# Three chained layers on one core: attention of the first token blocks spread over the matrix product's halves, old outputs copied out through the probabilities' buffer, weight pieces split in place

## The chip, the cores and the metric

The kernel runs on one core of a Trainium2 chip. The metric is the device time of one execution in microseconds (us), lower is better. Of a profiled execution the span (first to last instruction) is given too; the profile's times are counted from the span's start. The engines are PE (matrix products; PEld is its weight loading), DVE (VectorE), ACT (ScalarE), POOL (GpSimd) and SP (SyncE, which issues all DMAs of this kernel). Each engine takes its instructions strictly in the order of its own queue.

## The reference

```
q, k, v: (8, 8, 576, 64)                       # batch, heads, sequence, head size
k_p, v_p = means of k and v over groups of 8 in the sequence      # 72 rows a head
attn = softmax(q @ k_p.T / sqrt(64))           # 576 x 72 a head
x = (attn @ v_p), heads side by side           # 4608 tokens x 512
x = (sigmoid(x @ w_gate) * (x @ w_val)) @ w_out            # inner width 1536
h = x @ w_in2                                  # inner width 2048
out = where(h > 0, h, exp(min(h, 0)) - 1) @ w_out2         # 4608 x 512, float32
```

The inputs come as float64. The kernel narrows the weights to float32 with integer operations on VectorE, and keeps each float32 number as a high part (what TensorE takes) and a low rest, so that one product is three passes: high x high, high x low, low x high.

## The kernel before, in words

All of it is one function in which instructions are written in the order in which each engine takes them (the order is by hand; nothing is rescheduled). 4608 tokens are nine blocks of 512, each of four query tiles of 128. The stages, with names that the text uses:

**Stage 1 (begin).** Attention of block 0. For a query tile t: `emit_q` transposes the queries on PE and ACT copies them out; `emit_s` makes the scores on PE and `off_peak` subtracts each row's maximum on DVE (two instructions); `emit_exp` is ACT; `emit_norm` sums and inverts on DVE and scales on POOL; `emit_t` transposes the probabilities on PE, and ACT and DVE split them into `pt` (one buffer for the block). `emit_pv` multiplies them with the pooled values (`weighted`) and splits the result into `x`. `emit_k` and `sums_of` pool and place keys and values. Between these stand calls of `convert(1)`: one conversion is four DVE instructions on 128x512 (lines 109, 113, 119 and 123) that narrow one weight tile, an ACT absolute value (line 205) for the next one, and a split (ACT, then POOL, lines 96 and 97) of one before.

**Stage 2.** The loop over c = 0..5 of the first gated layer for block 0: a gate product (`emit_gate`, 12 matmuls), its sigmoid, a value product (12), `emit_g` (multiply on DVE, split), and for the c before, the output product (`emit_y`, 12). Three conversions lie in each c, and the attention of block 1 lies around the products. Every step of that attention takes the same pair of PSUM banks (`two_banks`, one buffer): scores, transposed queries and transposed probabilities wait for each other's readers. At its end `emit_pv(1)` makes `x` of block 1.

**Stage 3.** c = 6..11 of block 0, with block 1's gate and value products of two c's (`side_gate`, `side_val`) in each. `work(n)` lets a background generator (`form_weights`, then `prepared`) go on by n steps.

**Stage 4.** The output product of block 1, j = 0..9 (12 matmuls each), and the attention of block 2 around it, placed by `put2`; the last weight forms are stored. It ends with `weighted` of block 2.

**Stage 5.** Blocks 2 to 8 in a form with seven smaller products for eight: u = 0..11, each with seven steps k = 0..6 of six matmuls on 128x256. After each step some matmuls of the output product follow (`filler`), then what `thin_plan` put at (u, k): the attention of the next block in single banks (`q_thin`, `s_thin`, `t_thin`). `work()` is called at the places of `WORK_AT` (35 a block) and narrows the second layer's weights (`prepared`): tiles `a`, `b`, `c` of the tag `nt` (three buffers) and raw tiles of the tag `raw` (two buffers), which are stored to DRAM. `flush_one` copies the finished output of the block before to DRAM through the row tiles (three buffers, which the loads of q, k and v take too).

**Stage 6.** The second layer; PE is busy throughout, and the change doesn't touch it.

Of the kernel before, what the change touches and what calls it, by code (L numbers as in the profile page):

```python
# [24 lines left out]
def fused_kernel(  # L25
# [260 lines left out]
    def prepared():  # L286
# [21 lines left out]

        def store(d, place):
            nc.sync.dma_start(out=place, in_=f32(d))  # L310
# [17 lines left out]
        for q in range(C2 // 2):  # L328
# [31 lines left out]
            fetch(i + 3)  # L360
            yield
        last = None
        for i in range(C2, len(loads)):
            steps = narrowing(i)
            next(steps)
            if last is not None:
                store(last, wo2_dram[i - 1 - C2])
            yield
            next(steps)
            yield  # L370
            next(steps)
            if last is not None:
                fetch(i + 1)
            yield
            yield from steps
            last = halved(raws[i], tiles[i].bitcast(F32))
            yield
            magnitude(i + 1)
            yield
        yield  # L380
        yield
        store(last, wo2_dram[C2 - 1])
# [384 lines left out]
    def plan():  # L767


        early, pre, mid, post = [[[] for _ in range(C1)] for _ in range(4)]  # L770
        for i in range(TPW):
            t = TPW + i
            pre[1 + i].append(lambda t=t: (t, emit_s(t)))
            mid[2 + i].append(lambda t=t: emit_t(t))
        for i in range(TPW):
            pre[i].append(lambda t=TPW + i: emit_q(t))
        post[0].append(lambda: sums_of("v", 1))
        for c in range(NCH):
            post[(1, 1, 2, 3, 4)[c]].append(lambda c=c: place_v(1, c))
# [7 lines left out]
        return early, pre, mid, post  # L787

    with tc.manual_schedule():
# [51 lines left out]
        for c in range(NCH):  # L841
            pool_k(0, c)
        emit_k(0)
# [4 lines left out]
        open_to(2)  # L848
        scored(0)
        convert(1, 0, 0)  # L850
        scored(1)
        scored(2)
        emit_norm(0, ph[0])
        scored(3)
        emit_norm(1, ph[1])
        sums_of("v", 0)
        emit_t(0)
# [3 lines left out]
        convert(1, 1)  # L861
        emit_t(1)
# [3 lines left out]
        emit_t(2)  # L866
        sums_of("k", 1)
        convert(1, 1)
        emit_t(3)
        emit_pv(0)  # L870
        emit_k(1)
# [6 lines left out]
        early, pre, mid, post = plan()  # L878
# [10 lines left out]
        def side_gate(c):  # L889
            sg = at_p.tile([P, NW], F32, name="sg1", tag="qT" if c % 2 else "p")  # L890
            nc.scalar.activation(out=sg, in_=side(c, 0), func=AF.Sigmoid)
            return c, sg
# [8 lines left out]
        for c in range(C1):  # L901
            for f in early[c]:
                f()
            late = c >= LAG_FROM
            second = 2 * (c - LAG_FROM)
            later = [f for f in [op() for op in pre[c]] if f]
            gps = emit_gate(x0, c, 0)
            sg = emit_sig(gps)
            for f in later:
                emit_exp(f[1])  # L910
            convert(1)
            work(3)
            if late:
                one = side_gate(second)
            for op in mid[c]:
                op()
# [3 lines left out]
            for f in later:  # L920
                emit_norm(*f)
            for op in post[c]:
                op()
            if late:
                side_val(*one)
            convert(1)
            work(4)
# [5 lines left out]
            if late:  # L933
                side_val(*side_gate(second + 1))
                work(3)
                formed[0] = second // 2 + 1
            if c == LAG_FROM - 1:
                emit_pv(1)
                wide.close()
                lag_ps.append(lag.enter_context(tc.tile_pool(name="ps_lag", bufs=1, space=PSUM)))  # L940
# [16 lines left out]

        again(C1 - 2)
        while stores:
            stores.pop(0)[1]()  # L960
        reload(0)
        emit_k(SQ)
        emit_y(0, *pend)
# [5 lines left out]
        t0 = SQ * TPW  # L969
        emit_q(t0)  # L970
# [6 lines left out]
        at2 = [[] for _ in range(C1)]  # L977

        def put2(c, f, *a):
            at2[c].append(lambda: f(*a))  # L980
# [3 lines left out]
        def s2(t):  # L984
            p = raw_tile("p2").rearrange("p f w -> p (f w)").bitcast(F32)[:, :HK]
            p2[t] = emit_s(t, p)
            emit_exp(p)

        for i in range(TPW):
            t = t0 + i  # L990
            put2(2 * i, s2, t)
            put2(2 * i + 1, lambda t=t: emit_norm(t, p2[t]))
            if i + 1 < TPW:
                put2(2 * i, load_q, t + 1)
                put2(2 * i + 1, emit_q, t + 1)
            put2(2 * i + 3, emit_t, t)
        for c in range(NCH):
            put2((1, 2, 3, 4, 5)[c], load_kv, "k", SQ + 1, c)
            put2((4, 5, 6, 7, 8)[c], pool_k, SQ + 1, c)
        put2(8, emit_k, SQ + 1)  # L1000
        put2(9, load_q, t0 + TPW)
        for j, c in enumerate(order[:-2]):
            if j % 2 == 1:
                reload(j // 2 + 2)
            for f in at2[j]:
                f()
            y = y_steps(acc, g_of[c], c, wo[C1 + c], first=j == 0, last=False)
            for f in y:
                f()
# [3 lines left out]
            work(2)  # L1013
# [71 lines left out]
        a2 = two_banks("atv")  # L1085
# [563 lines left out]
```

## Time and profile before

| | us |
|---|---|
| runs, median of 3 (lowest to highest) | 1947.32 (1945.09 to 1948.89) |
| the profiled execution | 1951.63 |
| its span | 1949.9 |
| PE busy / DVE busy / ACT busy / POOL busy | 1812.7 / 1097.3 / 858.4 / 638.4 |
| stages 1, 2, 3, 4 | 58.9, 116.1, 119.9, 63.8 |
| stage 5, seven blocks | 131.6, 117.2, 118.8, 117.7, 114.3, 113.8, 112.2 |
| stage 6 | 765.7 |

The stages follow each other without overlap on PE, whose queue sets their order, so the span is their sum. PE is busy for 93% of the span; what it isn't busy, 137 us, lies nearly all in stages 1 to 5. A busy PE may also be a slow one: its clock has two levels, and the column PEclk of a window is the mean share of full speed that was granted in it.

### The profile page before, as it was taken

Reading aid. Unit: us, or ns where it says so; the run is one execution under the profiler, and the core shown is the slowest. Engines: PE = TensorE matmul, PEld = TensorE weight load, DVE = VectorE, ACT = ScalarE, POOL = GpSimd, SP = SyncE. Lnnn points to the kernel's source line nnn. Section 1 sums busy time; section 2 is a strip of 40 time slices with the busy share of each in tenths; the row PEclk is TensorE's granted clock in tenths of the full one; section 3 lists DMA queues with packets and bytes.
Section 4 is the critical chain, followed back from the end, with each engine's and each line's share of the span. In section 5 each row is a group of like instructions: output and inputs, shape, how many; then the busy total and the mean of one; then the engine's idle time right before and its main releaser. Section 6 shows DMA issues by size and latency. Waiting matters only on the chain. (4 is left out here: it accounts for less than half of the span.)

```text
span 1949.9 us, 28296 instructions
## 1 busy us (share of the span) xinstructions
PE 1812.7 (93%) x10308; PEld 1604.7 (82%) x10308; DVE 1097.3 (56%) x2053; ACT 858.4 (44%) x1775; POOL 638.4 (33%) x626
## 2 busy tenths in 40 slices
PE   5668997898999999999999999999999999999999
PEld 4556876688888888888889788999999999899898
DVE  6667985576676667766666554434444344443432
ACT  3343333344444444545444334444454444444443
POOL 2333564333334343333332322222222222222222
PEclk8778998899999999999999999999999999999999
DMA  8234545576676766666576786334343353343431
GB/s 221 90 114 131 195 159 190 202 232 206 218 231 204 253 211 211 222 230 224 179 250 209 267 291 260 130 121 171 114 178 114 116 190 126 131 172 133 146 114 52
DMA packets 158618, 351.29 MB, mean 180 GB/s; under 512 B 49168, under 2 KB 87056, under 8 KB 158480
## 3 DMA queue, kind: packets, MB, share of 16 engines
q1 hardware_dynamic: 158480, 349.48, 52.5%
q8 instruction: 82, 1.34, 0.3%
q14 instruction: 56, 0.46, 0.1%
HBM read 289.14 MB, written 60.29 MB: 179 GB/s over the span
## 5 line engine op out<-in xcount | busy, mean ns | idle before, releaser
L1480 PE MATMUL bank<-form,wr 128*128 128x384 f32 x2016 | 411.0, 338 | 1.0 <-DVE u L1513 0.7
L1480 PEld LDWEIGHTS bank<-form,wr 128*128 128x128 f32 x2016 | 366.5, 188 | 29.1 <-DVE u L1513 1.1
L717 PE MATMUL acc<-g,wos 128*128 128x512 f32 x1128 | 367.7, 409 | 22.5 <-ACT g L96 20.0
L1526 PE MATMUL oacc<-w2o,gc 128*128 128x512 f32 x1080 | 288.9, 393 | 0.4 <-POOL gc L97 0.4
L1526 PEld LDWEIGHTS oacc<-w2o,gc 128*128 128x128 f32 x1080 | 199.6, 187 | 30.4 <-POOL gc L97 0.8
L717 PEld LDWEIGHTS acc<-g,wos 128*128 128x128 f32 x1128 | 191.0, 195 | 39.3 <-ACT g L96 26.1
L97 POOL TENSOR_TENSOR gc<-ea,gc 128x384 fp32r<-128x384 f32 x96 | 98.1, 1022 | 298.5 <-ACT gc L96 293.2
L97 POOL TENSOR_TENSOR gc<-pair,gc 128x384 fp32r<-128x384 f32 x96 | 98.0, 1021 | 260.4 <-ACT gc L96 240.0
L1359 PE MATMUL pl<-s,wg 128*128 128x256 f32 x1008 | 155.4, 290 | 15.2 <-DVE u L1374 14.8
L1359 PEld LDWEIGHTS pl<-s,wg 128*128 128x128 f32 x1008 | 142.6, 192 | 31.9 <-DVE u L1374 16.5
L97 POOL TENSOR_TENSOR g<-sg,g 128x512 fp32r<-128x512 f32 x98 | 129.8, 1341 | 102.2 <-ACT g L96 102.0
L1359 PE MATMUL pl<-a,wg 128*128 128x256 f32 x1008 | 152.3, 287 | 6.6 <-ACT u L1369 4.1
L1359 PEld LDWEIGHTS pl<-a,wg 128*128 128x128 f32 x1008 | 142.0, 192 | 19.0 <-ACT r L1063 4.9
L1359 PE MATMUL pl<-s,tt 128*128 128x256 f32 x1008 | 153.9, 289 | 3.5 <-DVE u L1398 2.8
L1359 PEld LDWEIGHTS pl<-s,tt 128*128 128x128 f32 x1008 | 138.9, 191 | 12.2 <-DVE u L1398 3.9
L1526 PE MATMUL oacc<-w2p,gc 128*128 128x512 f32 x540 | 143.1, 393 | 0.0
L96 ACT ACTIVATE g<-sg 128x512 fp32r<-128x512 f32 x98 | 61.6, 628 | 151.0 <-DVE sg L1399 117.8
L1526 PEld LDWEIGHTS oacc<-w2p,gc 128*128 128x128 f32 x540 | 99.8, 187 | 14.8
L1489 ACT ACTIVATE ea<-bank 128x384 f32<-128x384 f32 x48 | 23.6, 492 | 157.3 <-PE bank L1480 157.3
L1493 DVE SCALAR_TENSOR_TENSOR ea<-ea,bank 128x384 f32<-128x384 f32 x48 | 26.6, 555 | 117.2 <-ACT ea L1490 117.2
L1394 POOL TENSOR_TENSOR sg<-sg,u 128x256 f32<-128x256 f32 x42 | 36.0, 858 | 162.6 <-DVE u L1393 162.6
L688 PE MATMUL gv<-x,wg 128*128 128x512 f32 x288 | 80.5, 436 | 3.6 <-DVE x L97 3.6
(225 smaller groups left out, 3075.9 us busy)
## 6 DMA issues: line engine op xcount, KB each, us to landing
wr<-wd SPq DMA_DIRECT2D x96, 896.0 KB, 6.5
tt<-td SPq DMA_DIRECT2D x84, 768.0 KB, 4.5
wos<-wd SPq DMA_DIRECT2D x94, 512.0 KB, 5.5
rw<-in_moe_w_out_dram SPq DMA_DIRECT2D x22, 512.0 KB, 3.9
td<-tw SPq DMA_DIRECT2D x36, 256.0 KB, 4.2
r<-yd SPq DMA_DIRECT2D x24, 384.0 KB, 8.2
out_dram<-po SPq DMA_DIRECT2D x36, 256.0 KB, 2.0
rw<-in_moe_w_in_dram SPq DMA_DIRECT2D x16, 512.0 KB, 6.2
```

Of the source, the lines that this page charges most:

```text
L96: nc.scalar.activation(out=dst_hi, in_=src, func=AF.Copy)
L97: eng.tensor_tensor(out=dst_lo, in0=src, in1=f32(dst_hi), op=ALU.subtract)
L688: nc.tensor.matmul(d, lhsT=w[:, i, a_w, j], rhs=x[j][:, a_x], start=(j == 0 and a_w == 0 and a_x == 0), stop=(j == KD - 1 and a_w == 1),)
L717: return lambda: nc.tensor.matmul(acc[m], lhsT=w[:, a_w, m * P:(m + 1) * P], rhs=g[:, a_g], start=(first and a_w == 0 and a_g == 0), stop= ...
L1359: nc.tensor.matmul(src, lhsT=w(a_w, j), rhs=f_t[nm][:, j, a_x], start=opens and m == 0, stop=m == 5, skip_group_check=True,)
L1394: nc.gpsimd.tensor_tensor(out=c22, in0=c22, in1=u4, op=ALU.mult)
L1480: nc.tensor.matmul(bank[b ^ flip], lhsT=wp[q][a_w][:, w, j * P:(j + 1) * P], rhs=form_tile(s, a)[j][:, a_x], start=opens and n == 0, stop= ...
L1489: nc.scalar.activation(out=e, in_=src, func=AF.Relu, scale=-1.0)
L1493: nc.vector.scalar_tensor_tensor(out=e, in0=e, scalar=-1.0, in1=src, op0=ALU.add, op1=ALU.max)
L1526: return lambda: nc.tensor.matmul(acc[t + i], lhsT=g[c][:, a_g, i * P:(i + 1) * P], rhs=wo2[2 * q + e][a_w], start=opens and p == 0, stop= ...
```

## The change

Six edits, named E1 to E6 in what follows.

**E1, stage 1.** The conversions move: one goes ahead of the keys' transposes, one behind the transposed probabilities, and one of five leaves the stage. All four score tiles come first, then the norms, then all four `emit_t`. `emit_k(1)` goes to stage 2.

**E2, stage 2.** The loops for c < 6 and c >= 6 are written apart. In c the order on PE is now: scores of tile t, gate, transposed probabilities of tile t-1, value, transposed queries of t+1, output. The output product of c = 5 follows `emit_pv(1)` and leaves stage 3.

**E3, stage 4.** A step j is cut into two halves of six matmuls, and `put2` places the attention by halves: queries, scores, exp, norm and transposes of a tile stand in different halves. The `weighted` products of block 2 move behind three more output matmuls, and what follows them (`form_x`) is spread over u = 0 as for the later blocks, no longer finished ahead of it.

**E4, stage 5, attention.** Nearly all of `thin_plan` moves one step k earlier; queries and values are loaded three to seven steps earlier than before.

**E5, stage 5, old outputs.** `flush_one` writes into a tile of the tag `pt`, which lies idle then, no longer into row tiles, and begins at (0, 3), before (0, 6).

**E6, `prepared`.** Splits of `c`, of `a`'s half and of the output weights are made in place (`apart`: the high part goes into another `nt` tile, the rest stays where the number was), where a raw tile took both parts. Each such piece is stored by two DMAs where one did it (24 more in all); raw tiles are fetched earlier. `WORK_AT` has 40 places a block, before 35.

```
+        def apart(x, r):
+            split(x.bitcast(F32R), r.bitcast(F32R), r)
...
-            dc = halved(raw_tile("rs2"), c)
             yield
             store(do, part(q, 1))
-            yield
-            store(dc, part(q, 2))
-            da = halved(raw_tile("rs2"), a[:, hi])
-            yield
+            apart(b, c)
+            yield
+            apart(a[:, lo], a[:, hi])
             fetch(i + 2)
             yield
-            store(da, part(q, 3, 1))
+            for n, x in enumerate((b, c)):
+                nc.sync.dma_start(out=w_dram[q][:, n, 4:6].rearrange("p a f -> p (a f)"), in_=x)
+            yield
+            nc.sync.dma_start(out=part(q, 3, 1), in_=a.rearrange("p (s f) -> p s f", s=2))
+            fetch(i + 3)
+            yield
             yield
             yield
             magnitude(i + 2)
-            fetch(i + 3)
             yield
...
+            fetch(i + 2)
+            last = plain_t().bitcast(F32), tiles[i].bitcast(F32)
+            apart(*last)
...
+        for c in range(LAG_FROM):
+            t = TPW + c - 1
+            p = emit_s(t) if 0 < c <= TPW else None
             gps = emit_gate(x0, c, 0)
+            if p is not None:
+                emit_exp(p)
             sg = emit_sig(gps)
             convert(1)
+            if c == 0:
+                emit_k(1)
+            elif c == 1:
+                sums_of("v", 1)
+            elif c <= TPW + 1:
+                emit_t(t - 1)
+            if p is not None:
+                emit_norm(t, p)
             vps = emit_gate(x0, c, 1)
             convert(1)
             g = emit_g(sg, vps)
             for op in post[c]:
                 op()
+            if c < TPW:
+                emit_q(t + 1)
             if pend is not None:
                 emit_y(0, *pend)
...
+        emit_pv(1)
+        emit_y(0, *pend)
...
+        for i, (hq, hs, ht) in enumerate(((0, 0, 5), (2, 3, 10), (7, 8, 15), (12, 13, 19))):
             t = t0 + i
+            if i:
+                put2(hq, emit_q, t)
+                put2(hq - 2, load_q, t)
+            put2(hs, s2, t)
+            put2(hs + 1, lambda t=t: emit_exp(p2[t]))
+            put2(hs + 2, lambda t=t: emit_norm(t, p2[t]))
+            put2(ht, emit_t, t)
...
-        filler(9)
-        for _ in shapes:
-            pass
...
+        filler(3)
+        d = places[:2] + [one_bank("atv")[:, 0, :], places[2]]
+        weighted(SQ, d)
+        shapes = form_x(SQ, d)
+        next(shapes)
+        filler(7)
...
-                put(u, 6, q_thin, t)
-                put(u + 1, 0, s_thin, t, 0)
-                put(u + 1, 2, s_thin, t, 1)
+                put(u, 5, q_thin, t)
+                put(u, 6, s_thin, t, 0)
+                put(u + 1, 1, s_thin, t, 1)
...
-                put(u, 0, load_q, t)
+                put(*((u - 1, 4) if i else (1, 1)), load_q, t)
...
-                        flush_one(n - 1, prev_acc, FLUSH_AT.index((u, k)), row_tile("yo"))
+                        m = FLUSH_AT.index((u, k))
+                        if m == 0:
+                            flushed = wts.tile([P, KD, NW], F32, name="yo", tag="pt")
+                        flush_one(n - 1, prev_acc, m, flushed[:, m])
+                        if m == KD - 1 and n + 1 < NWB:
+                            pt_now[0] = new_pt()
```

PE's queue in stage 2, one c, before (ats: scores, atq: transposed queries, att: transposed probabilities, gv: gate or value product, acc: output product):

```order
L574 MATMUL ats<-kbd_140,qT 128x144 x4
L566 MATMUL atq<-ident,q_173 128x128 x4
L688 MATMUL gv<-x,wg_738 128x512 x12
L628 MATMUL att<-ident,p_711 128x128 x4
L628 MATMUL att<-ident,pl 128x128
L688 MATMUL gv<-x,wg_738 128x512 x12
L717 MATMUL acc<-g,wo_683 128x512 x12
```

The same place now:

```order
L580 MATMUL ats<-kbd_140,qT 128x144 x4
L694 MATMUL gv<-x,wg_646 128x512 x12
L634 MATMUL att<-ident,p_572 128x128 x4
L634 MATMUL att<-ident,pl 128x128
L694 MATMUL gv<-x,wg_646 128x512 x12
L572 MATMUL atq<-ident,q_173 128x128 x4
L723 MATMUL acc<-g,wo_592 128x512 x12
```

Between any two steps that take the pair of banks there are now twelve matmuls of another kind; before, the transposed queries followed the scores directly.

PE's queue in stage 4, j = 2 and 3, before (wos: output weights):

```order
L717 MATMUL acc<-g,wos_2219 128x512 x12
L628 MATMUL att<-ident,p_2223 128x128 x4
L628 MATMUL att<-ident,pl 128x128
L566 MATMUL atq<-ident,rq 128x128 x4
L717 MATMUL acc<-g,wos_2221 128x512 x12
L574 MATMUL ats<-kbd_139,qT 128x144 x4
```

The same place now:

```order
L723 MATMUL acc<-g,wos_2219 128x512 x6
L634 MATMUL att<-ident,p_2223 128x128 x4
L634 MATMUL att<-ident,pl 128x128
L723 MATMUL acc<-g,wos_2219 128x512 x6
L723 MATMUL acc<-g,wos_2221 128x512 x6
L572 MATMUL atq<-ident,rq 128x128 x4
L723 MATMUL acc<-g,wos_2221 128x512 x6
L580 MATMUL ats<-kbd_139,qT 128x144 x4
```

Transposed probabilities and transposed queries stood side by side and have twelve matmuls between them now.

ACT's queue in stage 5 where `prepared` splits a piece, before (rw, rs: raw tiles; nt: narrowed tiles; u: the copy of the step k = 0 that the next products' sums need):

```order
L96 ACTIVATE rw_2817<-nt 128x512
L1387 ACTIVATE sg<-sg 128x256
L96 ACTIVATE rs_3202<-nt 128x512
L1390 ACTIVATE sg<-sg 128x512
L1146 ACTIVATE qT<-atq 128x512
L1369 ACTIVATE u_2750<-pl_2747 128x256
L501 ACTIVATE vhl<-vs 128x64
L1152 ACT_TABLE_LOAD
L1152 ACTIVATE idle<-idle 128x1
L600 ACTIVATE p<-p 128x576
L96 ACTIVATE rs_3291<-nt 128x256
```

The same place now:

```order
L96 ACTIVATE rw_2822<-nt 128x512
L1406 ACTIVATE sg<-pl_2637 128x256
L1409 ACTIVATE sg<-sg 128x256
L1167 ACTIVATE qT<-atq 128x512
L96 ACTIVATE nt<-nt 128x512
L1412 ACTIVATE sg<-sg 128x512
L96 ACTIVATE nt<-nt 128x256
L1391 ACTIVATE u_2640<-pl_2637 128x256
```

The splits of the second kind write `nt`, no longer a raw tile `rs` whose store has to land first.

## Rows read from the trace of the kernel before

**Rows 1.** Windows by stage: stages 1 to 4, blocks 2, 3, 7 and 8.

```profile
core 0: us, PE busy (x) PEld busy (x) DVE busy (x) ACT busy (x) POOL busy (x), PEclk, DMA share, GB/s
0.00:58.90 58.90, 34.13 (x170) 27.40 (x171) 33.89 (x58) 20.85 (x47) 15.36 (x27) 0.90 0.68 183
58.90:174.95 116.05, 78.75 (x358) 64.67 (x357) 81.98 (x116) 50.55 (x83) 43.98 (x34) 0.81 0.38 125
174.95:294.82 119.87, 117.60 (x505) 96.17 (x505) 93.95 (x132) 42.34 (x86) 63.42 (x56) 0.98 0.48 159
294.82:358.61 63.79, 49.32 (x210) 39.34 (x211) 36.17 (x59) 22.61 (x49) 27.04 (x23) 0.87 0.62 208
358.61:490.20 131.59, 117.28 (x778) 104.40 (x777) 82.15 (x171) 56.43 (x125) 45.73 (x49) 0.94 0.65 209
490.20:607.41 117.21, 109.78 (x770) 98.91 (x769) 82.83 (x170) 54.98 (x122) 44.48 (x46) 1.00 0.66 219
...
958.22:1072.02 113.80, 109.41 (x766) 98.95 (x765) 70.43 (x158) 53.55 (x109) 36.77 (x33) 1.00 0.63 213
1072.02:1184.20 112.18, 104.98 (x682) 94.93 (x681) 64.09 (x134) 38.23 (x86) 34.71 (x30) 0.95 0.77 275
```

**Rows 2.** Timeline of PE, stages 1 to 3; brackets: idle before, releaser.

```profile
48.47 0.49 PE L650 MATMUL atv<-pt,vbd 128*128 128x512 f32 x1 [1.80 <-ACT pt L96]
...
97.84 1.08 PE L566 MATMUL atq<-ident,q 128*128 128x128 f32 x4 [8.37 <-issue]
...
120.24 1.09 PE L566 MATMUL atq<-ident,q 128*128 128x128 f32 x4 [10.18 <-issue]
...
174.95 5.45 PE L688 MATMUL gv<-x,wg 128*128 128x512 f32 x12 [3.56 <-DVE x L97]
...
188.42 2.88 PE L717 MATMUL acc<-g,wo 128*128 128x512 f32 x12
```

**Rows 3.** Timeline of DVE, stages 1 and 2.

```profile
21.47 0.76 DVE L586 TENSOR_REDUCE mx<-ats 128x8 f32<-128x576 f32 x1 [6.46 <-PE ats L574]
...
23.54 0.42 DVE L109 TENSOR_SCALAR nt<-nt 128x512 f32<-128x512 f32 x1
...
107.28 0.69 DVE L97 TENSOR_TENSOR pt<-att,pt 128x512 fp32r<-128x512 f32 x1 [7.66 <-ACT pt L96]
...
119.38 0.76 DVE L587 TENSOR_TENSOR p<-ats,mx 128x576 f32<-128x576 f32 x1
```

**Rows 4.** Timeline of ACT, stage 2.

```profile
103.71 1.28 ACT L600 ACT_TABLE_LOAD   x1
...
106.67 0.58 ACT L96 ACTIVATE pt<-att 128x512 fp32r<-128x512 f32 x1
```

**Rows 5.** Groups by line, DVE, stage 2: count, busy us, mean ns, idle before.

```profile
L109 DVE TENSOR_SCALAR nt<-nt 128x512 f32<-128x512 f32 x15 | 13.7, 911 | 8.6 <-ACT nt L205 8.6
L113 DVE TENSOR_SCALAR nt<-nt 128x512 int32<-128x512 int32 x15 | 11.0, 731 | 0.0
L123 DVE SCALAR_TENSOR_TENSOR nt<-rwo,nt 128x512 int32<-128x512 int32 x9 | 8.1, 895 | 0.0
L119 DVE SCALAR_TENSOR_TENSOR nt<-rwo,nt 128x512 int32<-128x512 int32 x9 | 6.2, 684 | 0.1
```

**Rows 6.** Timeline of PE, block 2.

```profile
372.33 1.65 PE L1359 MATMUL pl<-a,wg 128*128 128x256 f32 x6 [4.12 <-ACT u L1369]
...
484.57 1.65 PE L1359 MATMUL pl<-s,wg 128*128 128x256 f32 x6 [3.66 <-DVE u L1374]
```

**Rows 7.** Timeline of ACT, block 2.

```profile
483.37 0.42 ACT L96 ACTIVATE rs<-nt 128x256 fp32r<-128x256 f32 x1 [5.63 <-DMA wd<-rw]
```

**Rows 8.** Waits of ACT, stage 5: total us, times, longest.

```profile
ACT rs L96 <- DMA wd<-rw: 19.2, 7, 5.6
...
ACT yo L749 <- DMA yd<-yo: 15.1, 4, 6.6
```

**Rows 9.** Waits of SP's queue, stage 5.

```profile
SPq L1024 <- PE pl L1359: 334.5, 68, 11.6
...
SPq L128 <- DMA wd<-rs: 36.1, 8, 7.5
```

**Rows 10.** Timeline of SP, block 8: the issue of one store.

```profile
1094.50 0.49 SPq L310 DMA_DIRECT2D wod<-rw  x1
```

More of the change, by code (lines that the diff above doesn't have):

```diff
@@ L359, in prepared, with keep @@
             magnitude(i + 2)
-            fetch(i + 3)
             yield
         last = None
+        def keep(i, x, y):
+            for n, z in enumerate((x, y)):
+                nc.sync.dma_start(out=wo2_dram[i - C2][:, n], in_=z)
         for i in range(C2, len(loads)):
@@ L366, in prepared @@
             if last is not None:
-                store(last, wo2_dram[i - 1 - C2])
-            yield
[L369 to L373, printed above, removed]
+                keep(i - 1, *last)
             yield
             yield from steps
-            last = halved(raws[i], tiles[i].bitcast(F32))
+            fetch(i + 2)
+            last = plain_t().bitcast(F32), tiles[i].bitcast(F32)
+            apart(*last)
             yield
@@ L381, in prepared @@
         yield
-        store(last, wo2_dram[C2 - 1])
+        keep(len(loads) - 1, *last)
     def background():
@@ L847, in fused_kernel @@
                 emit_q(t, qt[:, t], a[:, t - i, :])
[L848 to L855, printed above, removed]
+        for t in range(TPW):
+            scored(t)
+            if t > 1:
+                emit_norm(t - 2, ph[t - 2])
         sums_of("v", 0)
-        emit_t(0)
         emit_norm(2, ph[2])
@@ L865, in fused_kernel @@
             place_v(0, c)
-        emit_t(2)
+        for t in range(TPW):
+            emit_t(t)
+        convert(1, 1)
+        emit_pv(0)
         sums_of("k", 1)
[L868 to L871, printed above, removed]
         convert(1)
@@ L932, in fused_kernel @@
             pend = acc, g, c
[L933 to L940, printed above, removed]
+            convert(1)
+        emit_pv(1)
+        emit_y(0, *pend)
+        pend = None
+        wide.close()
+        lag_ps.append(lag.enter_context(tc.tile_pool(name="ps_lag", bufs=1, space=PSUM)))
+        for c in range(LAG_FROM, C1):
+            for f in early[c]:
+                f()
+            second = 2 * (c - LAG_FROM)
+            sg = emit_sig(emit_gate(x0, c, 0))
+            convert(1)
+            work(3)
+            one = side_gate(second)
+            vps = emit_gate(x0, c, 1)
+            convert(1)
+            g = emit_g(sg, vps)
+            for op in post[c]:
+                op()
+            side_val(*one)
+            convert(1)
+            work(4)
+            if pend is not None:
+                emit_y(0, *pend)
+            pend = acc, g, c
+            side_val(*side_gate(second + 1))
+            work(3)
+            formed[0] = second // 2 + 1
         lag.close()
@@ L956, in reload, with prep @@
                 back[2 * k], back[2 * k + 1] = t[:, 0], t[:, 1]
+        def prep(n=1):
+            for _ in range(n):
+                if stored[0] < C1:
+                    work()
         again(C1 - 2)
@@ L961, in fused_kernel @@
         reload(0)
+        t0 = SQ * TPW
         emit_k(SQ)
-        emit_y(0, *pend)
+        y = y_steps(pend[0], pend[1], pend[2], wo[pend[2]])
+        for f in y[:6]:
+            f()
+        emit_q(t0)
+        for f in y[6:]:
+            f()
         reload(1)
@@ L1083, in form_x @@
             yield
-        a2 = two_banks("atv")
-        d = [ps.tile([P, NW], F32, name="xv", tag="gv", bufs=2) for _ in range(2)] + [a2[:, 0, :], a2[:, 1, :]]
-        weighted(SQ, d)
-        shapes = form_x(SQ, d)
         fill = []
```

112 lines of the change are left out of this document (40 added, 72 removed).

## Prediction

> **What bounds the kernel now.** I read the windows by stage first: they tell where PE isn't busy and how fast its clock was. In stage 2 PE is busy for 78.75 of 116.05 us and the granted share is 0.81; in stage 4 it is 49.32 of 63.79 at 0.87; block 2 has 14.3 us of idle at 0.94, block 3 has 7.4 at 1.00, block 7 has 4.4, and block 8 has 7.2 at 0.95 [rows 1]. No other engine is full there: DVE has 82 us of work in stage 2, 36 in stage 4 and 82 in block 3. So these stages are bound by neither PE nor another engine, but by hand-overs between them. Stage 6 is PE without a gap, and the change leaves it alone.
>
> Then the timelines, for what ends the long waits. In stage 2 the transposed queries wait 8.37 and 10.18 us [rows 2]: they take the pair of banks that holds the scores, whose last reader on DVE starts at 119.38 and ends at 120.14 [rows 3], behind two conversions. PE stands with a gate product queued right behind. DVE is starved in its turn: at 107.28 it had waited 7.66 us for ACT, and ACT for PE. The two wait for each other once in each c. In block 2 PE waits 4.12 us for the first copy of ACT and 3.66 us at 484.57 [rows 6]; just before the latter ACT had waited 5.63 us for a store out of a raw tile [rows 7]. That wait comes 7 times in stage 5, 19.2 us together, and the copies of old outputs wait 15.1 us in 4 for their row tiles' stores [rows 8].
>
> **Stage 1 (E1).** A conversion is 0.91 + 0.73 + 0.90 + 0.68 = 3.2 us of DVE at stage 2's means [rows 5]; undisturbed, line 109 takes 0.42 rather than 0.91 [rows 3], so I put a conversion alone at twice 0.68 + 0.42, 2.2. Three conversions lay between the first scores (21.47) and the weighted sums (48.47) [rows 2, 3]. One moves ahead of the keys' transposes. I cost it at nothing: DVE sat idle 6.46 us before the first scores [rows 3]; without that cover it costs 2.2. One goes behind the transposed probabilities, beside PE's weighted sums; one goes to stage 2. The chain loses 6.6 to 9.7 us of DVE, of which the four splits of probabilities, now back to back with ACT between, take some. I take **-5.4**; bounds 0 and -9.7.
>
> **Stage 2 (E2).** Work is the same but for one key placement; DVE's 82 us are the floor and 116 the ceiling. What stays is one hand-over a c. When PE has transposed, ACT must first do what stands ahead: from the table load at 103.71 to the split at 106.67 it was 3.0 us [rows 4]. The 8 and 10 us waits go, since a gate or value product (2.88 us for twelve matmuls, [rows 2]) now lies between any two users of the banks. With some 3 us of starved DVE in each of six c's, 82 + 18 = 100, and 2 more for the last weighted sums and splits before stage 3: 102, so **-14**. It is nearer to the floor because the conversions that PE waited for now run while PE multiplies. Bounds -34 and 0.
>
> **Stage 3.** One output product (2.88 us) moves into the 3.56 us in which PE waited for `x`, and the first gate, 5.45 us after that wait, may run as the 2.88 of the later ones [rows 2]. DVE gets a conversion more (3.2 on 93.95 of 119.87, [rows 1]). **-4**; bounds 0 and -9.
>
> **Stage 4 (E3).** PE's 49.32 busy us at a granted 0.87 are about 43 at full clock [rows 1]. Its idle 14.5 us stand at transposes and scores that follow a sibling directly; these now have six or twelve matmuls between them. The transfers set a second floor: 208 GB/s for 63.8 us are 13.3 MB, and at block 8's 275 GB/s [rows 1] that is 48 us. I take 53, between the floor of 48 and the old time and nearer the floor, **-11**; bounds 0 and -16.
>
> **Block 2 (E3).** Its beginning becomes that of the later blocks, so its time becomes block 3's: 131.59 - 117.21 [rows 1] gives **-14**. The wait of 4.12 us and the slow clock behind it (1.65 us for six matmuls, at both long waits, [rows 6]) are what goes. The upper bound on the gain is block 7's time, -18; the lower, if the long wait at 484 us stays with what it costs in clock, -8.
>
> **Blocks 3 to 7 (E4, E5, E6).** Idle is 7.4 in block 3 and 4.4 in block 7. The store waits of ACT (rs and yo) go with their tiles, and SP's queue stands no longer for 36.1 us behind stores before it may fetch [rows 9], which let loads of queries and weights come late. In their place, the absolute value that follows a pair must now wait for the stores out of `nt`; there are three `work` steps between, where there was one. The 24 stores more cost 0.49 us of SP each [rows 10], 12 us in all; they are hidden because SP waits 334.5 us in stage 5 for PE to free a weight buffer [rows 9], and uncovered they would cost those 12 at most. Attention moves as a whole by one step, so its own spacing is kept. The preparing gets 40 steps for 35 a block and needs about 246 (seven more than before), so it ends with block 7; that makes earlier blocks denser on DVE by a seventh of the preparing. I take **-7** over five blocks; bounds +8 and -16.
>
> **Block 8.** Preparing leaves it; it had the largest share of DMA (0.77 at 275 GB/s, [rows 1]) and 7.2 us of idle, where block 7 has 4.4. **-4**; bounds 0 and -8.
>
> **Sum.** 5.4 + 14 + 4 + 11 + 14 + 7 + 4 = 59.4 us. The profiled execution took 1951.63 us (span 1949.9), so 1892.2 for such a one; it lay 4.3 above the median of the runs, so **1888 us**.
>
> **A rule against it.** DVE's instructions in stage 2 are longer than alone (0.91 for 0.42, [rows 5, 3]) while POOL works 43.98 us there. The Trainium skill, SBUF — State Buffer, section Who interferes with whom, says that a VectorE instruction with two SBUF inputs and a GpSimd one that reads SBUF exclude each other for their whole length. The trace agrees as far as that more than doubling goes. If all of POOL's work shut out all of DVE's, the floor of stage 2 would be 44 us plus DVE's undisturbed time, not 82: by my count 18 conversions of 2.2, four tiles of 3.7 (five instructions near 0.75) and some 8 of multiplications and splits, 62; together 106. I don't take it, since the instructions that read PSUM (subtracting the maximum, 0.76 in [rows 3], as the reduction before it in stage 1) show no lengthening.
>
> **Rivals.** (a) *DVE and POOL exclude each other:* stage 2 comes to 106 and, with the hand-overs left, to 114; stage 3's denser DVE eats its 4. Then -2 for -18: 1904. For it: DVE is busy 94 of 120 us in stage 3. Against it: DVE was idle for 34 us of stage 2, and the rows on that name ACT (7.66 once, 8.6 ahead of line 109, [rows 3, 5]). (b) *The blocks gain nothing:* the denser preparing costs what the tiles give, block 2 keeps its wait at 484 us: -8 for -25 over stage 5, 1905. For it: blocks with the heavy half of preparing are 3.4 us longer than block 7 [rows 1]. (c) *Slower:* ACT waits for stores out of `nt` as it did for raw tiles. There are 8 + 16 such pieces; the old wait was 19.2 / 7 = 2.7 us [rows 8]. If each holds ACT and PE with it, 24 x 2.7 = 65 us are lost and the result is about 1953; it decides from 2.5 us of PE a piece. Against it: three to five steps of slack for one, and PE lost only 3.66 of ACT's 5.63 us in the worst case. (d) *The order doesn't matter:* PE's waits go over to DVE's queue in all of stages 1, 2 and 4, as the conversions stay in order ahead of the subtractions; then -30 of -59 go, 1918.
>
> **Chances.** Forecast 0.62 (1870 to 1898), (a) 0.14, (b) 0.12, (d) 0.07, (c) 0.05. About 0.2% (4 us) is what a measurement of this kernel tells from no change. Faster 0.93, same 0.02, slower 0.05. The range reaches from 1866 (stage 2 near its floor, stage 4 at 48) to 1918, where (c) and the better tail are left out.
>
> **What would show it.** Stage 2 at 100 to 105 us with waits at transposed queries below 3 us, and DVE's wait for `pt` below 4; the first weighted sums at 43 us; stage 4 at 50 to 55 with no wait over 2 us; block 2 within 2 us of block 3; no ACT wait for a store at the copies of old outputs, and few at `nt`; block 8 with no fetch of output weights. The prediction is wrong if stage 2 stays over 110, or if ACT's waits for stores of `nt` exceed 20 us in stage 5.

## The result, and the profile after

The changed kernel takes 1871.92 us (median of 4 runs, 1869.42 to 1873.26); the kernel before took 1946.2 beside it (4 runs, 1939.94 to 1948.89). The ratio is 0.9621, 95% interval [0.9596, 0.9647]: 74 us faster, where 59 were forecast. 1888 was too high by 16 us; the time lies inside the range, near its lower end. The profiled execution took 1872.07 us, its span is 1869.8.

Windows by stage after, cut as in [rows 1]: stages 1 to 4, blocks 2, 3 and 8.

```profile
0.00:51.33 51.33, 32.37 (x161) 25.79 (x161) 29.86 (x55) 18.59 (x43) 11.51 (x25) 0.90 0.78 210
51.33:154.46 103.13, 82.32 (x378) 65.97 (x378) 79.88 (x115) 51.33 (x86) 45.85 (x34) 0.87 0.38 125
154.46:269.96 115.50, 112.69 (x493) 92.03 (x493) 98.97 (x136) 43.33 (x88) 65.92 (x57) 1.00 0.55 179
269.96:327.83 57.87, 43.94 (x214) 34.61 (x214) 38.39 (x60) 22.97 (x51) 27.68 (x24) 0.94 0.70 230
327.83:446.39 118.56, 111.10 (x775) 99.80 (x774) 79.06 (x170) 57.15 (x125) 44.48 (x49) 0.97 0.71 239
446.39:557.03 110.64, 108.80 (x770) 98.97 (x769) 82.42 (x174) 55.06 (x122) 43.64 (x46) 1.00 0.71 237
...
998.35:1104.13 105.78, 101.85 (x682) 92.42 (x681) 56.40 (x120) 33.59 (x78) 27.99 (x27) 0.98 0.70 256
```

The differences are -7.6, -12.9, -4.4 and -5.9 for stages 1 to 4, -13.0 for block 2 and -6.4 for block 8. Blocks 3 to 7 together, the sum row of the same five windows, before and then after:

```profile
sum 581.82, PE 549.61 PEld 493.89 DVE 391.38 ACT 273.88 POOL 210.75; mean PE 109.92 PEld 98.78 DVE 78.28 ACT 54.78 POOL 42.15
```

```profile
sum 551.96, PE 543.68 PEld 494.07 DVE 392.74 ACT 275.73 POOL 214.11; mean PE 108.74 PEld 98.81 DVE 78.55 ACT 55.15 POOL 42.82
```

That is -29.9. The seven numbers make -80.1, which is the span's 1949.9 - 1869.8; it is more than the 74 of the medians because the profiled execution of before was a long one. In blocks 3 to 7 PE's idle time (sum less PE busy) fell from 32.2 to 8.3 us, that is by 23.9; the other 5.9 is busy time for the same matmuls, and no row here says why it fell.

What ended PE's idle in those blocks, before (20 waits for ACT's split of `g`, the gated product):

```profile
PE acc L717 <- ACT g L96: 14.4, 20, 1.0
PE pl L1359 <- DVE u L1374: 6.7, 10, 1.4
PE atq L1145 <- DMA rq<-in_q_dram: 3.4, 4, 1.0
```

After, in the same blocks, 0.3 us of the first kind and none of the third is left:

```profile
PE pl L1381 <- DVE u L1396: 3.8, 4, 1.6
PE pl L1381 <- DVE xe L1078: 2.1, 5, 0.4
...
PE acc L723 <- ACT g L96: 0.3, 2, 0.2
```

Of the long waits that remain elsewhere, three matter in what follows. In stage 2, after's rows of PE, then of ACT, answer to [rows 2, 4]:

```profile
100.13 2.29 PE L580 MATMUL ats<-kbd,qT 128*128 128x144 f32 x8 [3.69 <-ACT qT L573]
```

```profile
98.96 0.63 ACT L96 ACTIVATE g<-sg 128x512 fp32r<-128x512 f32 x1 [4.00 <-DVE sg L712]
99.50 0.58 ACT L573 ACTIVATE qT<-atq 128x512 f32<-128x512 f32 x1
```

The scores wait for the copy of the queries, which stands on ACT behind a split that itself waits for DVE. It comes four times, 14.2 us together (longest 4.3). In stage 4, the timelines of SP (DMA issues) and PE:

```profile
274.20 4.75 SPq L760 DMA_DIRECT2D yd<-yo  x8
...
280.01 0.39 SPq L427 DMA_DIRECT2D rq<-in_q_dram  x1
```

```profile
286.77 1.08 PE L572 MATMUL atq<-ident,rq 128*128 128x128 f32 x4 [6.24 <-DMA rq<-in_q_dram]
```

PE waits 6.24 us for one query tile, whose load was issued behind eight stores of old outputs and two weight loads. In block 2, DVE waits for keys and PE for DVE:

```profile
357.16 1.01 DVE L483 TENSOR_REDUCE ks<-rkv 128x64 f32<-128x512 f32 x1 [4.70 <-DMA rkv<-in_k_dram]
```

```profile
358.56 1.65 PE L1381 MATMUL pl<-s,wg 128*128 128x256 f32 x6 [6.05 <-DVE u L1396]
```

### The profile page after: what moved, and what is told of

Its sections match the earlier page's. It is cut to its first block, busy times and chain, and to the rows that moved or that the text cites. A ratio compares the mean times of both kernels' runs of the same rounds, so it can differ in the third digit from the quotient of the medians.

```text
span 1869.8 us, 28366 instructions
## 1 busy us (share of the span) xinstructions
PE 1789.0 (96%) x10308; PEld 1588.6 (85%) x10308; DVE 1088.2 (58%) x2053; ACT 855.9 (46%) x1775; POOL 634.8 (34%) x626
## 4 chain that ended last, share of the span: by engine, by line
PE 78%; DVE 11%; ACT 4%; issue 2%; DMA 1%; POOL 0%; SPq 0%; DVEq 0%; POOLq 0%; ACTq 0%
PE oacc L1553 21%; PE bank L1507 19%; PE pl L1381 18%; PE acc L723 11%; PE gv L694 2%; PE ats L580 2%; PE gw L694 2%; PE pl L656 1%; DVE nt L109 1%; ACT L1173 1%; DVE nt L119 1%; DVE nt L123 1%; DVE tw L261 1%; DVE ks L483 1%; PE atq L1166 1%
## 5 line engine op out<-in xcount | busy, mean ns | idle before, releaser
L723 PE MATMUL acc<-g,wos 128*128 128x512 f32 x1128 | 355.4, 399 | 1.9 <-POOL g L97 0.7
L723 PEld LDWEIGHTS acc<-g,wos 128*128 128x128 f32 x1128 | 184.6, 190 | 13.4 <-ACT g L96 3.5
L1381 PE MATMUL pl<-s,wg 128*128 128x256 f32 x1008 | 153.6, 287 | 14.1 <-DVE u L1396 12.9
L1516 ACT ACTIVATE pair<-pair 128x384 f32<-128x384 f32 x48 | 25.2, 525 | 129.9 <-DVE pair L1537 129.9
```

The costliest lines, as they stand in the source:

```text
L723: return lambda: nc.tensor.matmul(acc[m], lhsT=w[:, a_w, m * P:(m + 1) * P], rhs=g[:, a_g], start=(first and a_w == 0 and a_g == 0), stop= ...
L1381: nc.tensor.matmul(src, lhsT=w(a_w, j), rhs=f_t[nm][:, j, a_x], start=opens and m == 0, stop=m == 5, skip_group_check=True,)
L1516: nc.scalar.activation(out=e, in_=src, func=AF.Relu, scale=-1.0)
```

## The experiments

The theory was that hand-overs decide: where a step stands in each queue (E1 to E5), and what a tile waits for before it may be written (E5, E6). The rivals were the prediction's (a) to (d). All ratios are to the kernel before. Windows of a stage that a run leaves as changed repeat well: stage 3 was 115.5 to 115.7 in all twelve runs and after, stage 2 was 102.2 to 103.1 wherever it is as changed. So a stage's window says what an edit did there, to about 1 us.

**u_q: one step of stage 2 put back.**

```
         p = emit_s(t) if 0 < c <= TPW else None
+        if 0 < c < TPW:
+            emit_q(t + 1)
         gps = emit_gate(x0, c, 0)
...
-        if c < TPW:
+        if c == 0:
             emit_q(t + 1)
```

> The changed kernel with one step of stage 2 put back: for c = 1 to 3 the transposes of the next queries stand right behind the scores again, as before; conversions and all else stay as changed. Theory X (the places in PE's queue decide, as in the prediction): three of the waits at transposed queries of 8 to 10 us come back, stage 2 takes 110 to 118 us instead of 103.1, and the time is 1879 to 1888. Theory Y (the prediction's rival d: the place doesn't matter, DVE's conversions set the pace either way): stage 2 stays within 3 us of 103, the time within 1868 to 1876.

1880.97 us (1878.02 to 1882.45), ratio 0.966 [0.964, 0.9679]. Stage 2's window:

```profile
49.93:162.55 112.62, 80.96 (x378) 65.24 (x378) 79.86 (x115) 51.64 (x86) 45.79 (x34) 0.88 0.35 115
```

Its waits, and one in the timelines of PE and DVE:

```profile
PE atq L572 <- issue: 15.2, 3, 7.7
```

```profile
109.74 1.09 PE L572 MATMUL atq<-ident,q 128*128 128x128 f32 x4 [7.71 <-issue]
```

```profile
102.13 1.75 DVE L123 SCALAR_TENSOR_TENSOR nt<-rwo,nt 128x512 int32<-128x512 int32 x1
...
104.73 0.68 DVE L119 SCALAR_TENSOR_TENSOR ntr<-rw,ntr 128x512 int32<-128x512 int32 x1
...
105.66 1.77 DVE L123 SCALAR_TENSOR_TENSOR ntr<-rw,ntr 128x512 int32<-128x512 int32 x1
107.35 0.83 DVE L113 TENSOR_SCALAR nt<-nt 128x512 int32<-128x512 int32 x1
108.11 0.74 DVE L592 TENSOR_REDUCE mx<-ats 128x8 f32<-128x576 f32 x1
```

Theory X holds: DVE's busy time is the same (79.86 for 79.88), yet the stage is 9.5 us longer. The transposed queries wait for the readers of the scores (line 592 and the one behind it), which stand on DVE behind the conversions (lines 109 to 123). The three waits are shorter than the 8 to 10 us that were expected, and they are not the whole of it: the scores' wait for ACT's copy falls from 14.2 to 4.3 us, and smaller waits come in other places. One step in another place is worth three quarters of what stage 2 gained; rival (d) falls for stage 2, and stages 1 and 4 had no run of this kind.

**b_q: ACT's copy of the queries ahead of the split of `g`.**

```
+        if c < TPW:
+            emit_q(t + 1)
         g = emit_g(sg, vps)
```

(and its old place dropped)

> The changed kernel, in stage 2 the transposes of the next queries written ahead of the gating's split, so that ACT copies them out before it splits g. In the changed kernel PE waits 14.2 us in four for that copy. Theory X (ACT's order sets that wait): it falls under 5 us, stage 2 to 91 to 96 us, and the time is 1859 to 1866. Theory Y (DVE's chain of conversions sets the pace of stage 2, and PE's wait moves elsewhere): stage 2 stays at 100 to 104, the time at 1868 to 1876.

1868.03 us (1864.85 to 1869.8), ratio 0.9594 [0.9574, 0.9613]; stage 2 took 101.69. Of the 14.2 us at the scores 0.7 are left, and PE now waits in the same stage for what DVE makes of the scores:

```profile
PE att L634 <- DVE p L593: 9.6, 3, 3.7
```

Theory Y holds: the wait went over to the next hand-over, and of 14 us 1.4 were won, hardly more than stage 2 differs between runs that leave it alone. Of the 22.3 us that PE is still idle in stage 2, these 9.6, where the scores' readers stand on DVE behind conversions, are the largest part; 5.4 are waits for POOL's splits of gate weights.

**b_load: the second query tile of stage 4 loaded earlier.** It goes into a raw tile, ahead of the old outputs' stores.

```
         emit_q(t0)
+        load_q(t0 + 1, raw_tile("rq2").rearrange("p f w -> p (f w)").bitcast(F32)[:, :512])
...
-                put2(hq - 2, load_q, t)
+                if i > 1:
+                    put2(hq - 2, load_q, t)
```

> The changed kernel with one load moved: the second query tile of block 2 goes ahead of the old outputs' stores, into a raw tile. In the changed kernel PE waits 6.24 us for it at the start of stage 4. Theory Q (that one load is late in SP's queue, behind eight stores and two loads): stage 4 gets 6 to 8 us shorter, the time 1863 to 1867. Theory T (stage 4 is bound by its transfers): under 3 us, 1869 to 1873, and another wait takes its place.

1867.84 us (1866.37 to 1869.97), ratio 0.9592 [0.9573, 0.9611]. Stage 4's window:

```profile
269.44:322.37 52.93, 44.21 (x213) 34.65 (x214) 37.62 (x60) 22.96 (x51) 27.71 (x24) 0.97 0.73 246
```

The wait of 6.24 us is gone, and the stage took 4.9 us less. By the medians the whole gained 4.1, between the two theories; its interval overlaps that of the changed kernel.

**b_first: no preparing step at u = 0 of block 2.**

```
-                    if (u, k) in WORK_AT:
+                    if (u, k) in WORK_AT and (n > SQ or u > 0):
```

> The changed kernel without the first preparing step of block 2 (that at u = 0); all later steps move back by one. In the changed kernel PE stands 6.05 us in block 2 because the next keys land late; their load was issued behind raw weights of 1 MB and eight stores of old outputs. Theory X (the raw weights hold it up): that stall falls under 3 us, block 2 to 112 to 115 us from 118.6, and the time is 1865 to 1869. Theory Y (the stores of old outputs hold it up): the stall stays over 5 us and the time at 1870 to 1875. Theory Z: preparing now lasts into block 8, and ACT and PE wait there for stores as in the run with 35 places: 1876 or more.

1872.98 us (1870.76 to 1875.23), ratio 0.9621 [0.96, 0.9641]: no difference. The stall was 5.10 us for 6.05. Blocks 3 to 7, though, took 558.33 us, 6.4 more than in the changed kernel. The raw weights were now issued 1 us behind the keys and no longer ahead of them, so their place ahead of the keys isn't what makes the stall; whether they still slow the keys' transfer isn't shown. The stores themselves were not moved in a run, so that the old outputs' stores make the stall is argued, not shown.

**b_all: b_q, b_load and b_first together.**

> The three together: the second query tile of block 2 loaded ahead of the old outputs' stores, ACT's copy of the queries ahead of the gating's split, no preparing step at u = 0 of block 2. If each gains what its theory X gives and they add up: 1852 to 1860. If only the load of the query tile gains: 1866 to 1870.

1868.17 us (1866.89 to 1868.8), ratio 0.9596 [0.9578, 0.9614]. Stages 2 and 4 took 100.22 and 53.09 us, but blocks 3 to 7 took 4.5 more than in the changed kernel (111.56, 112.16, 111.69, 110.07 and 110.99 us), with preparing one step later throughout. So the gains of b_q and b_load are there and b_first, which cost 6.4 us in these blocks alone, eats them. b_q with b_load alone was not run. Of the versions run, b_load and b_q are the fastest, 4 us below the changed kernel by the medians, with intervals that overlap its own.

**u_shift: the attention of stage 5 at its old steps.**

```
-                put(u, 5, q_thin, t)
-                put(u, 6, s_thin, t, 0)
-                put(u + 1, 1, s_thin, t, 1)
+                put(u, 6, q_thin, t)
+                put(u + 1, 0, s_thin, t, 0)
+                put(u + 1, 2, s_thin, t, 1)
...
```

> The changed kernel with queries, scores, norm and transposes of the next block one step k later again, at their old places; loads and everything else stay. Theory A (the norm at step 4 stood on DVE ahead of the subtraction and multiplication of step 5, whose result ACT splits for the output products): PE's wait for ACT's split comes back near 20 us over stage 5, and the time rises by 12 to 22 us, to 1884 to 1894. Theory S: under 4 us more, to 1876 at most.

1892.28 us (1888.86 to 1893.8), ratio 0.9715 [0.9694, 0.9737]. Theory A holds. Blocks 3 to 7 took 566.24 us, 14.3 more than after, block 2 5.4 more, and the waits for the split of `g` are back, though 13.2 us and not near 20 (stage 5):

```profile
PE acc L723 <- ACT g L96: 13.2, 23, 0.8
```

Timelines of the run's DVE and PE around one:

```profile
487.69 0.41 DVE L1418 TENSOR_TENSOR sg<-sg,pl 128x256 f32<-128x256 f32 x1
488.02 0.75 DVE L612 TENSOR_REDUCE sm<-p 128x8 f32<-128x576 f32 x1
...
489.94 1.21 DVE L1421 TENSOR_TENSOR sg<-sg,u 128x256 f32<-128x256 f32 x1
```

```profile
491.87 0.73 PE L723 MATMUL acc<-g,wos 128*128 128x512 f32 x2 [0.52 <-ACT g L96]
492.44 0.60 PE L634 MATMUL att<-ident,p 128*128 128x128 f32 x4
```

And the same place after, DVE, then PE:

```profile
483.90 0.74 DVE L612 TENSOR_REDUCE sm<-p 128x8 f32<-128x576 f32 x1
...
485.37 0.41 DVE L1418 TENSOR_TENSOR sg<-sg,pl 128x256 f32<-128x256 f32 x1
...
486.15 0.88 DVE L1421 TENSOR_TENSOR sg<-sg,u 128x256 f32<-128x256 f32 x1
```

```profile
486.96 0.60 PE L634 MATMUL att<-ident,p 128*128 128x128 f32 x4
487.32 0.96 PE L1381 MATMUL pl<-s,tt 128*128 128x256 f32 x6
488.12 0.63 PE L723 MATMUL acc<-g,wos 128*128 128x512 f32 x2
```

In u_shift, the sums of the next probabilities (line 612) stand on DVE between the two steps that finish the gated product (lines 1418 and 1421), and on PE the transposes stand behind the output product. After, the sums come before both steps, and the transposes stand ahead of the last six matmuls before the output product, which gives ACT more time. How much each of the two gives was not run apart.

**u_loads: the loads of queries and values, and the values' pooling and placing, at the old steps** (the attention stays one step earlier, so a load leads by less than before).

```
-                put(*((u - 1, 4) if i else (1, 1)), load_q, t)
+                put(u, 0, load_q, t)
...
-                    put(u - 1, 2, load_kv, "v", m, c)
-                    put(u + 1, 0, pool_v, m, c)
-                    put(u + 1, 2, place_v, m, c)
+                    put(u, 2, load_kv, "v", m, c)
+                    put(u + 1, 1, pool_v, m, c)
+                    put(u + 1, 3, place_v, m, c)
```

> The changed kernel with the loads of queries and values (and the pooling of values) at their old, later steps. Theory L (loads issued late let PE and DVE wait in each block): PE's waits for query tiles come back, 3 to 4 us in all, and DVE's for values; the time rises by 4 to 10 us, to 1876 to 1882. Theories S and A: under 4 us more.

1902.57 us (1899.23 to 1903.8), ratio 0.9763 [0.9743, 0.9782]: +31, far outside what was expected. Blocks 3 to 7 took 580.21. PE waits 11.7 us in 7 for queries there, the worst in block 5, and the matmuls behind it:

```profile
711.05 0.73 PE L1166 MATMUL atq<-ident,rq 128*128 128x128 f32 x4 [3.87 <-DMA rq<-in_q_dram]
711.44 1.63 PE L1381 MATMUL pl<-s,wg 128*128 128x256 f32 x6
```

Six matmuls took 1.63 us behind the wait; undisturbed ones of the same kind take 0.88. Windows of the stretches before, at and behind it:

```profile
700.00:711.00 11.00, 7.03 (x46) 5.88 (x44) 4.42 (x10) 3.20 (x8) 4.50 (x4) 1.00 0.95 281
711.00:715.40 4.40, 4.34 (x22) 4.18 (x23) 0.88 (x2) 1.78 (x3) 0.00 (x0) 0.61 1.07 404
715.40:726.00 10.60, 10.46 (x71) 9.09 (x71) 8.08 (x18) 4.92 (x9) 3.23 (x5) 1.00 0.45 160
```

The mean granted clock was 0.61 over the 4.4 us behind the wait, and 1.00 before and after; by an estimate that is 0.39 x 4.4 = 1.7 us on top of the wait. In these blocks PE's idle time rose by 15.5 us over after and its busy time by 12.8 (556.44 for 543.68). Seven waits at 1.7 would be 12 of the latter at most, but the block means of the clock, 0.99 to 1.00, show less; the rest stays open.

**u_rows: u_loads, and the old outputs through the row tiles again** (`flush_one` into `row_tile("yo")` at the new steps).

> The kernel of u_loads (late loads of queries and values) whose copies of old outputs go through the row tiles again, at their new steps. Theory R (the copies and the loads wait for each other's row tiles, and the new room took that away): ACT's waits for the copies' stores come back, some 15 us, and the time is 8 to 15 us over u_loads, 1910 to 1918. Theory N (the room matters little once the loads are late): within 4 us of u_loads, 1899 to 1906.

1901.02 us (1898.38 to 1902.44), ratio 0.976 [0.974, 0.978]: as u_loads, and theory R falls. ACT waits for no store at these copies in stage 5 here either, so with the copies at their new steps it isn't the room that took the 15.1 us [rows 8] away. The other room for old outputs gains nothing by itself with late loads. Row tiles with the early loads were not tried, so whether the room is what lets the loads go early is open.

**u_split: the old splits through raw tiles, the 40 new places kept** (`prepared` as before, `WORK_AT` as after).

> The changed kernel with the old splits of the second layer's weights (raw tiles take both parts, one store a piece); the 40 places for preparing, the attention's new steps and the new room for old outputs stay. Theory S (the stores out of raw tiles held ACT and SP, and so PE, in blocks 2 to 7): ACT's waits for raw tiles' stores come back near 19 us and the time rises by 12 to 22 us, to 1884 to 1894. Theory A (the attention's step was what delayed the gate's split): at most 5 us more, 1872 to 1877, and PE still waits under 3 us in all for ACT's split ahead of the output products. Theory L (late loads): at most 3 us more.

1887.59 us (1885.35 to 1889.57), ratio 0.9688 [0.967, 0.9707]: +16, as theory S has it. Blocks 3 to 7 took 569.15, 17.2 more than after. PE waits 21.3 us in 10 for DVE's `u` in stage 5, where it was 12.9 in 6, and ACT's waits for stores out of raw tiles are back there:

```profile
ACT rs L96 <- DMA wd<-rw: 19.3, 5, 7.7
```

**u_work: the 35 old places with the new splits.**

```
-        WORK_AT = {(u, k) for u in range(2, C1, 2) for k in (2, 3, 4, 5, 6)}
-        WORK_AT |= {(u, k) for u in range(3, C1, 2) for k in (2, 4)}
-        WORK_AT |= {(0, 5), (1, 1), (1, 3), (1, 5), (1, 6)}
+        WORK_AT = {(u, k) for u in range(2, C1, 2) for k in (1, 3, 4, 5, 6)}
+        WORK_AT |= {(u, 3) for u in range(1, C1, 2)} | {(0, 5), (1, 1), (1, 5), (1, 6)}
```

> The changed kernel with the old 35 places a block for preparing. The preparing then lasts into block 8. Theory S and theory A alike: block 8 gets back the 4 to 6 us that it lost, blocks 3 to 7 stay within 1 us each, so 1876 to 1879. If the placing itself (odd u: steps 2 and 4, before step 3) is what took the waits away, blocks 3 to 7 get 4 to 6 us longer each and the time is 1890 or more.

1925.22 us (1920.96 to 1928.63), ratio 0.9881 [0.9857, 0.9904]: +53, which neither theory had. Blocks 3 to 7 took 564.19, 12.2 more than after, but block 8 with what follows up to the second layer took this:

```profile
1006.01:1151.57 145.56, 110.33 (x674) 98.86 (x672) 69.76 (x140) 37.55 (x85) 34.41 (x30) 0.86 0.60 210
```

ACT's waits there, one in its timeline, and PE behind it:

```profile
ACT nt L301 <- DMA wod<-nt: 30.8, 4, 8.9
```

```profile
1104.32 0.66 ACT L301 ACTIVATE nt<-rw 128x512 f32<-128x512 f32 x1 [7.96 <-DMA wod<-nt]
```

```profile
1105.76 1.65 PE L1380 MATMUL pl<-s,wg 128*128 128x256 f32 x6 [6.51 <-DVE u L1395]
```

With 35 places preparing lasts into block 8, and there the absolute value of the next piece (line 301) waits for the stores out of `nt`: rival (c)'s mechanism, at 7.7 us a time instead of the 2.7 that it was priced at. ACT's copies for PE are queued behind it.

**u_e6: all of E6 undone** (old splits and old places).

> The changed kernel with both the splits and the 35 places of before, so all of the preparing as it was. Theory C (the two edits belong together: with 35 places the preparing lasts into block 8, where the transfers are late, and tiles split in place then hold ACT for their stores): without tiles in place those waits can't come, so 1885 to 1896, far below the 1925 of u_work. Theory W (35 places cost by themselves): 1925 or more.

1884.68 us (1883.85 to 1885.58), ratio 0.9678 [0.9656, 0.9699]: +13 for the whole, where each half undone alone gave +16 (u_split) and +53 (u_work). Against u_e6, with neither, the splits in place alone cost 40 us and the 40 places alone gain nothing (+3, within the intervals); both together gain 13. So the two need each other.

**u_all5: E4, E5 and E6 undone together, the beginning of block 2 as changed** (but the old numbers of output matmuls behind the steps of u = 0 and 1, `Y_FIRST`, which the change had altered too).

> Stages 1 to 4 and the start of block 2 as changed, all of stage 5's attention, loads, old outputs, splits and places as before. If the parts' prices add (16 + 53 + 20 + 31 us for the four undone alone), 1992. If each undone part alone makes a mismatch with the others, the time is what the windows of blocks 3 to 8 say: 1872 + 30 + 6 = 1908, give or take 5; PE then waits again near 20 us for ACT's split and near 15 for DVE.

1906.68 us (1905.93 to 1908.71), ratio 0.9792 [0.9773, 0.9811]: +35. Blocks 3 to 7 took 579.98, within 2 us of before. So these edits together carry 28.0 of the 29.9 us in these blocks. Undone singly, the attention's steps cost 14.3 there, E6 9.5 (561.44) and the loads 28.3, 52.1 in all: the prices don't add, and none of them is an edit's share of the 28.0.

## Why the prediction was right, and where it was off

**What bounds it** was right for the kernel before: the gain came from hand-overs, and DVE has nearly the same work in stage 2 and in blocks 3 to 7 after. In stages 1, 2 and 4 no engine is full after either; in blocks 3 to 7 PE now nearly is, busy 543.68 of 551.96 us. The time lies inside the range although one term missed by 22.9 us; that stage 4 missed by 5.1 the other way kept it above 1870, and that is luck.

**Stage 1** gave -7.6 for -5.4, the first weighted sums at 39.52 for 43. It is inside the bounds; that the conversions that moved were worth a little more than I took is argued, since no run took it apart.

**Stage 2** gave -12.9 for -14 and 103.13 us, in the 100 to 105 named. The mechanism is shown by u_q. PE's waits at the transposed queries are down to 1.0 us in all, and the scores now wait 3.6 us each (14.2 in 4) for ACT's copy. The sum took 20 us of idle DVE in the stage; it was 23.3 (103.13 - 79.88). b_q shows that taking the scores' waits away brings others of like length (9.6 in 3) for DVE.

**Rival (a)** falls as a price, not as a mechanism. The stage ran under its floor of 106, by 3 us. But single instructions do behave so: in u_q's rows above line 123 took 1.75 and 1.77 us, where line 119, which reads two tiles of SBUF too, took 0.68. POOL, in the same stretch of the run:

```profile
101.89 1.44 POOL L97 TENSOR_TENSOR wg<-nt,wg 128x512 fp32r<-128x512 f32 x1
105.61 1.27 POOL L97 TENSOR_TENSOR g<-sg,g 128x512 fp32r<-128x512 f32 x1 [2.29 <-ACT g L96]
```

Both long ones end about 0.5 us after POOL's instruction, and the short one lies where POOL is idle. The Trainium skill, SBUF — State Buffer, section Who interferes with whom, says the same of such pairs. The trace agrees: of line 123's 18 instances in that stage, the ten that start while POOL is in an instruction take 1.75 to 1.79 us, the other eight 0.68 or 0.69. The doubling that the prediction set beside that rule, though, was line 109's, which has one SBUF input; it too took 1.37 to 1.52 us when it started beside POOL (7 of 18) and 0.41 or 0.42 otherwise. And that readers of PSUM aren't lengthened was no reason against it, since the conversions read SBUF. What failed in (a) was to add up all of POOL's work, 45.9 us after, as if all of it met DVE's. The four conversion lines take 64.1 us in stage 2 after, and would take 40.7 at their undisturbed 0.42 and 0.68; so by this estimate some 23 of DVE's 79.9 us there are lengthening beside POOL. No run took POOL's work out of stage 2, so what that costs the stage stays open.

**Stage 3** gave -4.4 for -4. No run took it apart.

**Stage 4** gave -5.9 for -11 and 57.87 us, outside the 50 to 55 named, with one wait far over 2 us. The step that failed is that only siblings on PE were counted, and the DMA queue was not. The load of the second query tile has the same place in SP's queue as before, behind eight stores and two weight loads. Before, its issue and the transposes that need it:

```profile
303.42 0.39 SPq L421 DMA_DIRECT2D rq<-in_q_dram  x1
```

```profile
309.11 0.63 PE L566 MATMUL atq<-ident,rq 128*128 128x128 f32 x4 [1.20 <-DMA rq<-in_q_dram]
```

There the scores ahead of it had waited 3.23 us for ACT, and PE came to the transposes 4.5 us after the issue and waited 1.20. After, the scores don't wait, PE was ready 0.5 us after the issue (286.77 - 6.24, for 280.01) and waited 6.24. With the load ahead of the stores b_load gives 52.93, where 53 was forecast; the missing 5 are this load. That it comes so near 53 is luck in part: 53 was chosen between the old time and a floor of 48, and the 275 GB/s of that floor is no limit, since the kernel before moved 334 GB/s over 50 us of block 8 (1102 to 1152).

**Block 2** gave -13.0 for -14, but it is not within 2 us of block 3, since block 3 fell too and a stall of 6.05 us for late keys took the place of the 4.12 and 3.66 us ones [rows 6]. So that -13.0 came so near -14 is luck: two errors, the stall and the fall of block 3, cancelled. My lower bound had a long wait that stays, but another one.

**Blocks 3 to 7** gave -29.9 for -7, outside my bounds of +8 and -16: this is the term that was mis-sized, and at 22.9 it is more than the whole error (80.1 for a sum of 59.4). Two steps failed. "Attention moves as a whole by one step, so its own spacing is kept" looked at the attention alone; what counted is where its sums and transposes fall between the gated product and the output product that waits for it, 14.4 us of PE in 20 waits which I had not read from the waits of these blocks. u_shift shows it: +14.3. And ACT's waits for raw tiles' stores were priced by what PE lost directly; undoing E6 costs 9.5 in these blocks. The loads, undone alone, cost 28.3, so how the 29.9 divide among the edits isn't shown; u_all5 shows that together they make 28.0 of it. I had the right measure in front of me: the idle time of blocks 3 and 7, 7.4 and 4.4 us [rows 1]. It was 32.2 over five blocks, 23.9 of it went, and I took 7.

**Rival (b)** falls (the blocks gained most), and **(c)** did not happen: ACT waited for a store out of `nt` once in stage 5, 1.6 us. But its mechanism is real, as u_work shows; it is kept away by preparing that is over early in block 8 (its last stores are issued at 1024.83, 26 us into it).

**Block 8** gave -6.4 for -4, inside the bounds. It fetches no raw weights any more, as forecast; no run took it apart otherwise.

## What to carry to other kernels

When work moves past a hand-over, price the whole idle time of the stage, by what ends it, and not only the waits that name the edited tiles; and follow each load into the queue that issues it. A step's place in a queue can be worth 9 us with nearly the same work on each engine (u_q), but taking away one wait can merely show the next one (b_q: 1.4 of 14), and a faster order can uncover a load that was hidden (stage 4). Edits that lean on each other must be undone together to be priced: half of E6 undone alone (u_work) cost four times as much as all of it.

## What was not expected of the hardware

Stores kept ACT waiting for their tiles longer than the 2.7 us a time read before: 7.7 us a time (30.8 in 4) for stores out of `nt` in block 8 of u_work, where the DMA share was 0.60, and 3.9 (19.3 in 5) for those out of raw tiles in u_split. After idle times of 3.9 to 6.5 us on PE (u_loads, after, u_work), the next six matmuls took 1.63 to 1.65 us for the usual 0.88, as in block 2 before [rows 6]. The mean granted clock was 0.61 over the next 4.4 us of u_loads, between the lower level (half, 1.2 GHz) and full (1.00, 2.4 GHz).
